# Attention on one Trainium2 core: score and transpose products grouped by PSUM bank, and casts of q and k given new places

## The chip, the core and the metric

The kernel runs on one core of one Trainium2 chip. The core has five engines that run side by side, each with its own queue of instructions in program order: TensorE (PE in the rows; PEld is its weight load), VectorE (DVE), ScalarE (ACT), GpSimd (POOL) and SyncE (SP), which here only starts DMAs. An instruction waits for others by semaphores. TensorE writes to PSUM, which is divided into banks of 128 x 512 float32; VectorE and ScalarE read them. The metric is device microseconds of one execution. 785.85 us is the median of three runs before (785.13 to 787.29).

## The reference, cut to what matters

```python
scores = 1 / sqrt(64) * (q @ k.T)                # 4 batches, 8 heads, 576 x 64
cum = cumsum(log(clip(f, 1e-4, 1)))
scores = where(causal, -1e9, scores + cum[:, None] - cum[None, :])
attn = exp(scores - scores.max(-1))
attn = attn / (attn.sum(-1) + 1e-9)
x = (attn @ v)                                   # 2304 tokens x 512
# then: each token to the best of 8 experts (x normalised), relu(x @ w1) @ w2, times the gate
# then: max of three products, times w_out
```

All in float32. The change lies in the attention alone.

## The kernel before

**Pairs and heads.** Attention goes through 16 pairs of heads `p`, two heads `h = 2p, 2p+1` each, four pairs to a batch. For a pair SyncE loads `q2` and `k2` (128 x 1152, L251). A score product in full precision is made of high and low parts: `q_hi` and `k_hi` cast to the rounded type fp32r (L315, L318, by `evict`: L433 on VectorE, L435 on ScalarE), GpSimd subtracts the casts from the originals (`q_lo` L321 into `At`, `k_lo` L324 into `R2`), SyncE copies `At` to `Bt` (L327). Three sets of these buffers (`At`, `Bt`, `R1`, `R2`) are in turn, so the split for pair `p` runs while the heads of earlier pairs are computed.

**A head.** The 576 rows of a head are five blocks `t` of 64, 128, 128, 128, 128 rows; by causality block `t` needs 64, 192, 320, 448, 576 columns. For each block there are two score products (L344: `At` by `R1`, and `Bt` by `R2`) into a PSUM bank `s`; block 4 is cut in two of 288 columns, so a head has six `s` tiles, with three banks in turn. VectorE's reduction (L361, a custom instruction followed by a read of its accumulator) adds the mask, writes `P` and the row extreme `nm`, which frees the bank. ScalarE's `exp` (L381) follows. TensorE transposes `P` by 128 x 128 (L397), the last 64 columns of each block into a bank `tl` (L393, L399), and the first 64 x 64 (L401); VectorE or ScalarE copies each bank `t` (two in turn) and `tl` (one) to `PT` (L433, L435).

**A pair's output.** When both heads are transposed, two groups `po` (L459) multiply `PT` by `v`; `ot` (L469) copies the result, `pb` (L478) transposes it back, L487 normalises it with `rs` (L445), and SyncE stores it. At the end of a batch a chain of small VectorE instructions and a few products (L575 ff., `ohp` L724, `pr`, `ptab`) routes the tokens.

**What sets the order.** The code does not write instructions in one order. It lists tasks with an engine (or a choice of two), a planned cost, a priority, and the tasks they need; `Sched` (L122) takes, again and again, the task that could start first by its own clock, the priority breaking ties, and emits its instructions. So the queues' order is decided when the kernel is built, by planned costs. The tasks' dependencies steer that order alone; the semaphores in the built program come from the data that instructions read and write. PSUM banks are planned by `get` and `rel`: a tile is taken by the task with `get` and given back by the one with `rel`. The order of blocks in a head is `order = (4, 0, 3, 1, 2)`, and products have a width of at least 192 columns (`wp`, L342), also for block 0, which needs 64.

Of the kernel before, what the change touches and what calls it, by code (L numbers as in the profile page):

```python
# [214 lines left out]
def attention(tc, g, qT, kT, v, x_dram, es):  # L215
# [87 lines left out]

    def split_tasks(p):
        i, u = p % NQ, 10 * p - 6
        load = None
        if p > 1:
            old = [fs[h, t, k] for h in (2 * p - 6, 2 * p - 5) for t in range(NBLK) for k in range(1 + (t == 4))] if p >= NQ else []
# [27 lines left out]
    def s_task(h, t, k, j0, w):  # L336
        p, r = divmod(h, 2)
        i = p % NQ

        def fn(e):  # L340
            st = st_[h, t, k] = ps_s.tile([128, 512], F32, tag="s", name=f"s_{h}_{t}_{k}")
            wp = max(w, 192)  # L342
            for ps_i, (lt, rt, kk) in enumerate(((At[i], R1[i], 128), (Bt[i], R2[i], 66))):
                nc.tensor.matmul(st[:, 0:wp], lt[0:kk, r, ROW0[t]:ROW0[t] + 128],  # L344
                                 rt[0:kk, r, j0:j0 + wp], start=(ps_i == 0), stop=(ps_i == 1))

        fs[h, t, k] = sd.task("PE", pe(2 * max(w, 192)), fn, slot[h, t] - LEAD, ready[p], get=("s", (h, t, k)))

    def r_task(h, t, k, j0, w, n, ext):
        def fn(e):  # L350
            if k == 0:
                if t == order[0] and h % H == 0:
                    b = h // H
# [12 lines left out]
        fr[h, t] = sd.task("DVE", dve(w), fn, slot[h, t], deps, get=None if k else ("P", (h, t)), rel=[("s", (h, t, k))])

    def head(h):
        p, r = divmod(h, 2)
        b = h // H  # L370
        T = PT[h % NPT]
        for t in order:
            n, ext = ROWS[t], EXT[t]
            parts = ((0, 288), (288, 288)) if t == 4 else ((0, ext),)
            for k, (j0, w) in enumerate(parts):
                s_task(h, t, k, j0, w)
                r_task(h, t, k, j0, w, n, ext)

            def exp(e, t=t, n=n, ext=ext, k=len(parts) - 1):
                P, nm = Pt[h, t]  # L380
                nc.scalar.activation(out=P[0:n, 0:ext], in_=P[0:n, 0:ext], func=AF.Exp, bias=nm[0:n, k:k + 1], scale=-1.0,  # L381
                                     accum_out=sums[b][0:n, t, h % H:h % H + 1])

            fe[h, t] = sd.task("ACT", 0.28 + ext / 1200, exp, slot[h, t], [fr[h, t]])
        old = [fo[p - 2, u] for u in range(2)] if p >= 2 else []
        for t in order:
            i0 = ROW0[t]

            def tr(e, t=t, i0=i0):
                P = Pt.pop((h, t))[0] if t not in (0, 4) else Pt[h, t][0]  # L390
                if t == 0:
                    tl = tl_[h] = ps_t.tile([128, 512], F32, tag="tl", name=f"tl_{h}", bufs=1)
                    nc.tensor.transpose(tl[0:64, 384:512], Pt.pop((h, 4))[0][:, 512:576], g.ident)  # L393
                    return
                w = tl_[h, t] = ps_t.tile([128, 512], F32, tag="t", name=f"t_{h}_{t}")
                for a in range(t):
                    nc.tensor.transpose(w[:, 128 * a:128 * a + 128], P[:, 128 * a:128 * a + 128], g.ident)  # L397
                if t != 4:
                    nc.tensor.transpose(tl_[h][0:64, 128 * t - 128:128 * t], P[:, 128 * t:128 * t + 64], g.ident)  # L399
                if t == 1:  # L400
                    nc.tensor.transpose(w[0:64, 128:192], Pt.pop((h, 0))[0][0:64, 0:64], g.ident[0:64, 0:64])  # L401

            nb = {0: 1, 1: 2.5, 2: 3, 3: 4, 4: 4}[t]
            deps = [fe[h, t]] + ([fe[h, 4]] if t == 0 else [ft[h, 0]] if t != 4 else [])
            ft[h, t] = sd.task("PE", 0.107 * nb, tr, slot[h, t] + LT, deps, get=("tl", h) if t == 0 else ("t", (h, t)),
                               rel=[("P", (h, x)) for x in {0: (4,), 1: (0, 1), 4: ()}.get(t, (t,))])
            if t == 0:
                continue

            def ev(e, t=t, i0=i0):  # L410
                w = tl_.pop((h, t))
                if t == 1:
                    evict(e, T[0:64, 0, 0:64], w[0:64, 128:192])
                evict(e, T[:, 0:t, i0:i0 + 128], w[:, 0:128 * t].rearrange("p (a i) -> p a i", a=t))

            x = 0.13 if t == 1 else 0.0
            fv[h, t] = sd.task(("ACT", "DVE"), (act(128 * t) + x, dve(128 * t) + x), ev, slot[h, t] + LT - 4, [ft[h, t]] + old,
                               rel=[("t", (h, t))])

        def tail(e):  # L420
# [1039 lines left out]
```

## Time and profile before

| | before |
|---|---|
| median of 3 runs | 785.85 us (785.13 to 787.29) |
| the profiled execution, and its span | 785.06 us, 783.3 us |
| busy: TensorE, VectorE, ScalarE, GpSimd | 738.9 us (94%), 461.9 (59%), 368.2 (47%), 237.7 (30%) |
| the chain that ended last, share by engine | TensorE 75%, VectorE 9%, DMA 7%, issue 4%, others 1% or less each |
| granted TensorE clock, mean | 0.984 of full speed |
| attention | about 10 to 221 us; then routing and experts |

The shares are averages over stages with different limits. Attention takes the first 28% of the span; there VectorE and ScalarE are nearly as busy as TensorE, while behind 242 us TensorE works almost alone. A "busy" TensorE says that products follow each other; from the distance of two starts (the pitch) one reads what a product costs, since the listed time of one includes its passage through the array. The clock is the share of full speed that the chip granted. In rows with `[x <-E tile Lnn]` the engine had been idle for x us before, until engine E's instruction released it.

### The profile page before, as it was taken

The page shows a single profiled execution, that of the slowest core. Times are in us where ns is not written, and L with a number is a line of the kernel's source. Part 1 is how long each engine was busy: PE and PEld are TensorE (multiplying, and loading weights), DVE is VectorE, ACT ScalarE, POOL GpSimd, SP SyncE. Part 2 cuts the span into 40 slices and gives each one's busy share as a digit, 9 for nine tenths or more (in the row PEclk, how much of TensorE's full clock was granted, in tenths as well). Part 3 has the DMA queues.
Part 4 walks back from the last instruction along what each step waited for, and adds up shares of the span by engine and source line. Part 5 has one row for each costly group of instructions (what it writes and reads, how often), then busy time and mean ns, then how long its engine had stood idle before and what let it go on. Part 6 is the DMA issues. An engine that isn't in the chain of part 4 may idle for free.

```text
span 783.3 us, 13403 instructions
## 1 busy us (share of the span) xinstructions
PE 738.9 (94%) x4862; PEld 682.3 (87%) x4862; DVE 461.9 (59%) x1076; ACT 368.2 (47%) x870; POOL 237.7 (30%) x189
## 2 busy tenths in 40 slices
PE   2989999999949998999999999999999999999996
PEld 1868877778738998999999999989999899999995
DVE  6888887988567998867767877941211211112110
ACT  5668887978836653454554563231211212212111
POOL 7464443532020344234223113341221211212112
PEclk9999999999978999999999999999999999999998
DMA  9959775751145465556474653200000000100001
GB/s 228 239 125 216 191 178 143 182 118 40 23 116 208 151 220 181 186 181 233 151 257 147 230 198 126 82 28 14 1 40 1 28 14 1 41 0 15 28 1 43
DMA packets 44614, 90.19 MB, mean 115 GB/s; under 512 B 23320, under 2 KB 23320, under 8 KB 44544
## 3 DMA queue, kind: packets, MB, share of 16 engines
q1 hardware_dynamic: 40960, 77.83, 34.0%
q0 software_dynamic: 3152, 9.88, 3.5%
q10 hardware_dynamic: 432, 1.57, 0.5%
q8 instruction: 40, 0.66, 0.3%
q14 instruction: 30, 0.25, 0.1%
HBM read 74.97 MB, written 9.44 MB: 108 GB/s over the span
## 4 chain that ended last, share of the span: by engine, by line
PE 75%; DVE 9%; DMA 7%; issue 4%; ACT 1%; POOL 1%; SPq 1%; POOLq 0%; DVEq 0%; ACTq 0%
PE pm L907 10%; PE pm L906 10%; PE pm L908 10%; PE s L344 6%; PE po L459 6%; PE t L397 4%; PE ph L908 3%; PE ph L907 3%; PE py L906 3%; PE py L908 3%; PE ph L906 3%; PE py L907 3%; PE po L1268 3%; PE po L1267 3%; PE po L1266 3%
## 5 line engine op out<-in xcount | busy, mean ns | idle before, releaser
L1240 DVE TENSOR_TENSOR tm<-pm,tm 128x384 f32<-128x384 f32 x72 | 40.1, 557 | 199.4 <-PE pm L908 198.2
L907 PE MATMUL pm<-x_y,m 128*128 128x384 f32 x432 | 144.5, 335 | 0.0
L908 PE MATMUL pm<-x_y,m 128*128 128x384 f32 x432 | 144.4, 334 | 0.0
L906 PE MATMUL pm<-x_y,m 128*128 128x384 f32 x432 | 144.4, 334 | 0.0
L381 ACT ACTIVATE P<-P,nm 128x576 f32<-128x576 f32 (+4 forms) x160 | 88.3, 555 | 17.0 <-DVE nm L361 16.7
L344 PE MATMUL s<-R,At 128*128 128x192 f32 (+1 forms) x192 | 71.3, 380 | 14.9 <-DVE At L271 10.5
L934 ACT ACTIVATE w<-stg 128x1024 fp32r<-128x1024 f32 x63 | 66.2, 1056 | 33.3 <-DMA stg<-in_w_dram 14.4
L907 PEld LDWEIGHTS pm<-x_y,m 128*128 128x128 f32 x432 | 81.1, 188 | 0.6 <-POOL x_y L1199 0.3
L951 DVE TENSOR_TENSOR w<-stg,w 128x1024 fp32r<-128x1024 f32 x54 | 70.2, 1304 | 19.3 <-ACT w L934 18.9
L907 PE MATMUL ph<-x,w 128*128 128x384 f32 (+7 forms) x256 | 79.3, 310 | 2.1 <-DVE x L1083 2.1
L906 PEld LDWEIGHTS pm<-x_y,m 128*128 128x128 f32 x432 | 81.1, 188 | 0.2
L908 PEld LDWEIGHTS pm<-x_y,m 128*128 128x128 f32 x432 | 81.1, 188 | 0.0
L906 PE MATMUL py<-h,w 128*128 128x384 f32 (+7 forms) x256 | 79.5, 311 | 0.8 <-DVE h L1141 0.8
L908 PE MATMUL ph<-x,w 128*128 128x384 f32 (+7 forms) x256 | 79.4, 310 | 0.8 <-DVE w L951 0.7
L906 PE MATMUL ph<-x,w 128*128 128x384 f32 (+7 forms) x256 | 79.4, 310 | 0.7 <-ACT x L934 0.7
L1251 POOL TENSOR_TENSOR g<-tm,g 128x384 fp32r<-128x384 f32 x34 | 36.5, 1074 | 141.4 <-ACT g L934 141.4
L908 PE MATMUL py<-h,w 128*128 128x384 f32 (+7 forms) x256 | 78.5, 307 | 0.4 <-DVE w L951 0.4
L907 PE MATMUL py<-h,w 128*128 128x384 f32 (+7 forms) x256 | 78.2, 305 | 0.0
L934 ACT ACTIVATE g<-tm 128x384 fp32r<-128x384 f32 x36 | 18.8, 524 | 115.9 <-DVE tm L1240 115.9
L361 DVE CUSTOM_DVE_ANT_0 P<-s,mask 128x288 f32<-128x288 f32 (+4 forms) x160 | 64.4, 422 | 11.1 <-PE s L344 6.7
L344 PE MATMUL s<-R,Bt 66*128 66x192 f32 (+1 forms) x192 | 60.2, 320 | 4.3 <-DMA R<-clo 4.3
L321 POOL TENSOR_TENSOR At<-q,At 64x1152 fp32r<-64x1152 f32 x15 | 40.3, 2684 | 77.1 <-DVE At L433 24.7
(246 smaller groups left out, 1620.4 us busy)
## 6 DMA issues: line engine op xcount, KB each, us to landing
stg<-in_w_dram SPq DMA_DIRECT2D x61, 512.0 KB
q<-in_q_dram SPq DMA_DIRECT2D x32, 288.0 KB
k<-in_k_dram SPq DMA_DIRECT2D x32, 288.0 KB
sd<-in_m_dram SPq DMA_DIRECT2D x18, 512.0 KB
Bt<-At SPq DMA_DIRECT2D x16, 288.0 KB
v<-in_v_dram SPq DMA_DIRECT2D x4, 1024.0 KB
x_dram<-XL SPq DMA_DIRECT2D x64, 64.0 KB
sd_o<-in_mo_dram SPq DMA_DIRECT2D x6, 512.0 KB
```

What stands on the lines that cost most here:

```text
L321: nc.gpsimd.tensor_tensor(out=At[i][64:128], in0=raws[p][0][64:128], in1=At[i][64:128].bitcast(F32), op=ALU.subtract)
L344: nc.tensor.matmul(st[:, 0:wp], lt[0:kk, r, ROW0[t]:ROW0[t] + 128], rt[0:kk, r, j0:j0 + wp], start=(ps_i == 0), stop=(ps_i == 1))
L361: nc.vector.tensor_tensor_reduce(out=P[0:n, j0:j0 + w], in0=st_.pop((h, t, k))[0:n, 0:w], in1=g.mask[0:n, m0:m0 + w], scale=-0.125, scalar ...
L381: nc.scalar.activation(out=P[0:n, 0:ext], in_=P[0:n, 0:ext], func=AF.Exp, bias=nm[0:n, k:k + 1], scale=-1.0, accum_out=sums[b][0:n, t, h % ...
L459: nc.tensor.matmul(po[64 * r:64 * r + 64, lo - c0:w], vt[b][0:n, a, (2 * hp + r) * D:(2 * hp + r + 1) * D], PT[(2 * p + r) % NPT][0:n, a, ...
L906: nc.tensor.matmul(out, whi, xhi, start=start, stop=False)
L907: nc.tensor.matmul(out, whi, xlo, start=False, stop=False)
L908: nc.tensor.matmul(out, wlo, xhi, start=False, stop=stop)
L934: nc.scalar.activation(out=out, in_=in_, func=AF.Copy)
L951: ENG[e].tensor_tensor(out=w[:, 1], in0=t, in1=w[:, 0].bitcast(F32), op=ALU.subtract)
L1240: nc.vector.tensor_tensor(out=mx[0], in0=mx["p", w][:, 0:MC], in1=mx[0], op=ALU.max)
L1251: ENG[e].tensor_tensor(out=ht[:, 1, :], in0=mx[0], in1=ht[:, 0, :].bitcast(F32), op=ALU.subtract)
```

## The change

Three things, all in `attention()`.

*Scores by bank.* A head has four units in place of six tiles: block 4's first half, its second half, blocks 2 and 1 side by side in one bank (320 + 192 columns), blocks 3 and 0 in one bank (448 + 64). Block 0's products are 64 columns wide and no longer 192. Of the two blocks in a bank the second is reduced first, and the bank is given back behind the other.

*Transposes by bank.* Three groups, block 4, blocks 2 and 1, blocks 3 and 0, each into one `t` bank. A group waits for the exponentials of both its blocks; the bank `tl` is begun right ahead of block 4's group. The copies to `PT` are as many as before.

*Casts.* The planned costs of a cast go from (1.02, 0.67) to (1.1, 0.8), those of a subtraction from 2.6 to 2.7. In the plan `q_lo` now needs both casts, `k_lo` needs `q_lo`, and the casts of a pair need the `k_lo` of the pair before (`quiet`).

```diff
-        qh = sd.task(("ACT", "DVE"), (1.02, 0.67), q_hi, u, old + [load])
-        ql = sd.task("Pool", 2.6, q_lo, u, [qh])
+        qh = sd.task(("ACT", "DVE"), (1.1, 0.8), q_hi, u, old + [load, quiet[0]])
         qc = sd.task("SP", 0.9, q_copy, u, [qh], lat=2.0)
-        kh = sd.task(("ACT", "DVE"), (1.02, 0.67), k_hi, u, old + [load])
-        kl = sd.task("Pool", 2.6, k_lo, u, [kh])
+        kh = sd.task(("ACT", "DVE"), (1.1, 0.8), k_hi, u, old + [load, quiet[0]])
+        ql = sd.task("Pool", 2.7, q_lo, u, [qh, kh])
+        kl = quiet[0] = sd.task("Pool", 2.7, k_lo, u, [kh, ql])
...
+    UNITS = (((4, 0, 0, 288, 0),), ((4, 1, 288, 288, 0),), ((2, 0, 0, 320, 0), (1, 0, 0, 192, 320)), ((3, 0, 0, 448, 0), (0, 0, 0, 64, 448)))
+    FLIPS = ((4,), (2, 1), (3, 0))
...
+            for t, k, j0, w, c in UNITS[n]:
+                for ps_i, (lt, rt, kk) in enumerate(((At[i], R1[i], 128), (Bt[i], R2[i], 66))):
+                    nc.tensor.matmul(st[:, c:c + w], lt[0:kk, r, ROW0[t]:ROW0[t] + 128], rt[0:kk, r, j0:j0 + w],
+                                     start=(ps_i == 0), stop=(ps_i == 1))
...
+        for x, (t, k, j0, w, c) in enumerate(UNITS[n][::-1]):
...
+            end = x == len(UNITS[n]) - 1
+            dep = fr[h, t] = sd.task("DVE", dve(w), red, u, [dep] + ([fr[h, t]] if k else []), get=None if k else ("P", (h, t)),
+                                     rel=[("s", (h, n))] if end else [])
...
+    def slot(h, n):
+        return 5 * h + (0, 0.5, 1.5, 3)[n]
...
+            ft[h, n] = sd.task("PE", cost, tr, u + LT, [fe[h, t] for t in ts] + [ft[h, "tl"]], get=("t", (h, n)),
+                               rel=[("P", (h, t)) for t in ts])
...
-            ts = (0, 1, 2) if u == 0 else (0, 3, 4)
+            ts = (1, 2, "tl") if u == 0 else (0, 2, "tl")
```

The numbers of instructions on TensorE, of reductions and of copies to `PT` are the same in both. What moves, in three places; in the names a first number is the head (or the pair, for `q2`, `k2`, `po`, `ot`), a second the block before and the unit or the first block of a group after.

VectorE, before, around the casts of pairs 3 and 4 (`P` and `s` are of head 4, `ISA` is the reduction and, in the row behind it, its accumulator read):

```order
L361 ISA P_4_1_577,nm_4_1_578<-s_4_1_0_555,mask_81 128x192
L361 ISA nm_4_1_578 128x1
L433 CAST R10_116<-k2_3_414 128x1152
L487 TENSOR_TENSOR XL0_599<-pb_0_0_573,rs_0_441 128x3x144
L445 TENSOR_SCALAR rs_1_605<-sums0_205 128x10
L446 RECIPROCAL rs_1_605<-rs_1_605 128x10
L433 CAST At1_111<-q2_4_506 128x1152
L433 CAST R11_117<-k2_4_507 128x1152
L433 COPY PT3_125<-tl_3_558 64x4x64
```

VectorE, after, around the casts of pair 4:

```order
L447 COPY PT0_122<-tl_4_616 64x4x64
L447 CAST At1_111<-q2_4_555 128x1152
L365 ISA P_6_4_706,nm_6_4_707<-s_6_0_695,mask_81 128x288
L365 ISA nm_6_4_707 128x1
L447 CAST R11_117<-k2_4_556 128x1152
L365 ISA P_6_4_706,nm_6_4_707<-s_6_1_709,mask_81,nm_6_4_707 128x288
```

The cast of `k` of pair 3 has left VectorE (it stands on ScalarE); those of pair 4 come two heads later, with one reduction between them.

VectorE, before, from the cast of `q` of pair 10 on (heads 15 and 16):

```order
L433 CAST At1_111<-q2_10_1514 128x1152
L361 ISA P_16_4_1681,nm_16_4_1682<-s_16_4_1_1676,mask_81,nm_16_4_1682 128x288
L361 ISA nm_16_4_1682 128x1
L361 ISA P_16_0_1716,nm_16_0_1717<-s_16_0_0_1697,mask_81 64x64
L361 ISA nm_16_0_1717 64x1
L361 ISA P_16_3_1719,nm_16_3_1720<-s_16_3_0_1701,mask_81 128x448
L361 ISA nm_16_3_1720 128x1
L433 CAST R11_117<-k2_10_1515 128x1152
L433 COPY ot_6_0_1730<-po_6_0_1709 128x320
L433 COPY PT3_125<-t_15_3_1725 128x3x128
```

VectorE, after, at the same casts:

```order
L447 CAST At1_111<-q2_10_1499 128x1152
L365 ISA P_16_1_1663,nm_16_1_1664<-s_16_2_1632,mask_81 128x192
L365 ISA nm_16_1_1664 128x1
L365 ISA P_16_2_1673,nm_16_2_1674<-s_16_2_1632,mask_81 128x320
L365 ISA nm_16_2_1674 128x1
L459 TENSOR_SCALAR rs_7_1679<-sums1_877 128x10
L460 RECIPROCAL rs_7_1679<-rs_7_1679 128x10
L447 CAST R11_117<-k2_10_1500 128x1152
L365 ISA P_16_0_1705,nm_16_0_1706<-s_16_3_1684,mask_81 64x64
L365 ISA nm_16_0_1706 64x1
L365 ISA P_16_3_1708,nm_16_3_1709<-s_16_3_1684,mask_81 128x448
```

The two casts stand as far apart as before, but the copy `ot` no longer follows the cast of `k`; it is on ScalarE, behind the exponential of block 3.

TensorE, before, from the second half of block 4 of head 16:

```order
L344 MATMUL s_16_4_1_1676<-R12_118,At2_112 128x288
L344 MATMUL s_16_4_1_1676<-R22_121,Bt2_115 128x288
L397 MATMUL t_15_4_1684<-ident_78,P_15_4_1611 128x128 x4
L344 MATMUL s_16_0_0_1697<-R12_118,At2_112 128x192
L344 MATMUL s_16_0_0_1697<-R22_121,Bt2_115 128x192
L344 MATMUL s_16_3_0_1701<-R12_118,At2_112 128x448
L344 MATMUL s_16_3_0_1701<-R22_121,Bt2_115 128x448
L393 MATMUL tl_15_1705<-ident_78,P_15_4_1611 64x128
```

TensorE, after, from the same products:

```order
L349 MATMUL s_16_1_1628<-R12_118,At2_112 128x288
L349 MATMUL s_16_1_1628<-R22_121,Bt2_115 128x288
L349 MATMUL s_16_2_1632<-R12_118,At2_112 128x320
L349 MATMUL s_16_2_1632<-R22_121,Bt2_115 128x320
L349 MATMUL s_16_2_1632<-R12_118,At2_112 128x192
L349 MATMUL s_16_2_1632<-R22_121,Bt2_115 128x192
L392 MATMUL tl_15_1645<-ident_78,P_15_4_1566 64x128
L409 MATMUL t_15_4_1647<-ident_78,P_15_4_1566 128x128 x4
L409 MATMUL t_15_2_1656<-ident_78,P_15_2_1605 128x128 x2
L392 MATMUL tl_15_1645<-ident_78,P_15_2_1605 64x128
L409 MATMUL t_15_2_1656<-ident_78,P_15_1_1597 128x128
```

Four products in a row now fill one bank, and the transposes of two blocks stand together; what came between them (single tiles of 192 or 448 columns, single blocks) stands earlier or later.

## Rows read from the trace of the kernel before

**Rows 1.** Stretches: from:to us; length, busy us of engines (instructions), PEclk, DMA share, GB/s

```profile
47.60:51.20 3.60, 3.60 (x15) 2.87 (x16) 2.35 (x11) 2.04 (x6) 3.52 (x2) 0.53 1.02 248
62.00:99.00 37.00, 37.00 (x309) 30.23 (x308) 31.91 (x118) 32.38 (x106) 16.57 (x7) 1.00 0.83 198
```

**Rows 2.** Waits of TensorE, 44.9 to 221.4 us: total us, times, longest

```profile
PE s L344 <- DVE nm L361: 4.1, 3, 2.4
PE pb L478 <- DVE ot L433: 1.7, 2, 0.9
```

**Rows 3.** Line 433, casts of k: durations ns min/median/max, first and last start

```profile
L433 DVE CAST R<-k x13: 747/2168/3074, 40.2 to 177.7; 128x1152 fp32r<-128x1152 f32 x13
```

**Rows 4.** Timeline from 39 us: start, duration us, engine, line, out<-in [idle before]

```profile
39.50 2.63 POOL L321 TENSOR_TENSOR At<-q,At 64x1152 fp32r<-64x1152 f32 x1 [6.62 <-DVE nm L361]
...
40.25 2.50 DVE L433 CAST R<-k 128x1152 fp32r<-128x1152 f32 x1
...
43.51 2.63 DVE L433 CAST At<-q 128x1152 fp32r<-128x1152 f32 x1
...
46.06 0.75 DVE L433 CAST R<-k 128x1152 fp32r<-128x1152 f32 x1
...
46.27 3.04 POOL L321 TENSOR_TENSOR At<-q,At 64x1152 fp32r<-64x1152 f32 x1 [0.75 <-issue]
...
47.60 0.46 PE L344 MATMUL s<-R,At 128*128 128x192 f32 x1 [2.38 <-DVE nm L361]
```

**Rows 5.** Timeline, a cast on ScalarE

```profile
28.06 1.15 ACT L435 ACTIVATE R<-k 128x1152 fp32r<-128x1152 f32 x1
```

**Rows 6.** Timeline, casts of pair 9

```profile
101.89 3.07 DVE L433 CAST R<-k 128x1152 fp32r<-128x1152 f32 x1
...
105.16 0.41 PE L344 MATMUL s<-R,At 128*128 128x320 f32 x1 [0.84 <-DVE nm L361]
```

**Rows 7.** Timeline from 114 us, casts of pair 10

```profile
114.02 1.20 PE L459 MATMUL po<-PT,v 128*64 128x320 f32 x12
114.03 2.64 POOL L321 TENSOR_TENSOR At<-q,At 64x1152 fp32r<-64x1152 f32 x1 [6.29 <-PE s L344]
...
114.93 2.35 DVE L433 CAST R<-k 128x1152 fp32r<-128x1152 f32 x1
...
117.20 0.48 DVE L433 COPY ot<-po 128x320 f32<-128x320 f32 x1
...
117.73 1.00 PE L478 MATMUL pb<-w,ot 128*128 128x144 f32 x6 [0.83 <-DVE ot L433]
118.67 2.10 PE L459 MATMUL po<-PT,v 128*64 128x256 f32 x20
```

**Rows 8.** Groups by line and shape in attention: busy us, mean ns, idle before

```profile
L361 DVE CUSTOM_DVE_ANT_0 P<-s,mask 128x448 f32<-128x448 f32 x32 | 19.7, 615 | 2.7 <-PE s L344 1.3 <-ACT P L381 0.6
L381 ACT ACTIVATE P<-P,nm 128x448 f32<-128x448 f32 x32 | 21.2, 662 | 0.5 <-DVE nm L361 0.2
L724 DVE TENSOR_TENSOR ohp<-iota,rm 128x640 f16<-128x640 f32 x3 | 2.5, 826 | 0.0
```

**Rows 9.** Timeline of TensorE at 62 us: pitches

```profile
62.32 0.27 PE L344 MATMUL s<-R,Bt 66*128 66x192 f32 x1
62.43 0.27 PE L397 MATMUL t<-ident,P 128*128 128x128 f32 x1
62.54 0.27 PE L399 MATMUL tl<-ident,P 128*64 128x128 f32 x1
62.74 0.24 PE L401 MATMUL t<-ident,P 64*64 64x64 f32 x1
62.91 0.42 PE L344 MATMUL s<-R,At 128*128 128x320 f32 x1
```

**Rows 10.** Timeline at the start of attention

```profile
14.51 2.62 POOL L321 TENSOR_TENSOR At<-q,At 64x1152 fp32r<-64x1152 f32 x1
...
16.04 0.46 DVE L361 CUSTOM_DVE_ANT_0 P<-s,mask 128x288 f32<-128x288 f32 x1 [1.58 <-PE s L344]
```

More of the change, by code (lines that the diff above doesn't have):

```diff
@@ L307, in split_tasks @@
         if p > 1:
-            old = [fs[h, t, k] for h in (2 * p - 6, 2 * p - 5) for t in range(NBLK) for k in range(1 + (t == 4))] if p >= NQ else []
+            old = [fs[h, n] for h in (2 * p - 6, 2 * p - 5) for n in range(4)] if p >= NQ else []
             load = sd.task("SP", 3.3, lambda e: load_pair(p), u - 8, ready[p - 2], lat=2.0)
@@ L334, in split_tasks, with s_unit @@
+        ql = sd.task("Pool", 2.7, q_lo, u, [qh, kh])
+        kl = quiet[0] = sd.task("Pool", 2.7, k_lo, u, [kh, ql])
         ready[p] = [x for x in (qh, ql, qc, kh, kl, dec) if x is not None]
-    def s_task(h, t, k, j0, w):
+    UNITS = (((4, 0, 0, 288, 0),), ((4, 1, 288, 288, 0),), ((2, 0, 0, 320, 0), (1, 0, 0, 192, 320)), ((3, 0, 0, 448, 0), (0, 0, 0, 64, 448)))
+    FLIPS = ((4,), (2, 1), (3, 0))
+    def s_unit(h, n):
         p, r = divmod(h, 2)
[L338 to L353, printed above, removed]
+        b, i = h // H, p % NQ
+        u = slot(h, n)
+        def mm(e):
+            st = st_[h, n] = ps_s.tile([128, 512], F32, tag="s", name=f"s_{h}_{n}")
+            for t, k, j0, w, c in UNITS[n]:
+                for ps_i, (lt, rt, kk) in enumerate(((At[i], R1[i], 128), (Bt[i], R2[i], 66))):
+                    nc.tensor.matmul(st[:, c:c + w], lt[0:kk, r, ROW0[t]:ROW0[t] + 128], rt[0:kk, r, j0:j0 + w],
+                                     start=(ps_i == 0), stop=(ps_i == 1))
@@ L354, in fn, with red @@
+        cost = 0.08 + sum(2 * max(0.112, 0.013 + x[3] / 2400) for x in UNITS[n])
+        dep = fs[h, n] = sd.task("PE", cost, mm, u - LEAD, ready[p], get=("s", (h, n)))
+        for x, (t, k, j0, w, c) in enumerate(UNITS[n][::-1]):
+            def red(e, t=t, k=k, j0=j0, w=w, c=c):
+                if n == 0 and h % H == 0:
                     sums[b] = sm.tile([128, NBLK, H], F32, tag="sums", name=f"sums{b}", bufs=2)
                     nc.vector.memset(sums[b][64:128, 0, :], 1.0)
-                P = pp.tile([128, S], F32, tag="P", name=f"P_{h}_{t}")
@@ L365, in r_task @@
-        deps = [fs[h, t, k]] + ([fr[h, t]] if k else [])
-        fr[h, t] = sd.task("DVE", dve(w), fn, slot[h, t], deps, get=None if k else ("P", (h, t)), rel=[("s", (h, t, k))])
+                if k == 0:
+                    P = pp.tile([128, S], F32, tag="P", name=f"P_{h}_{t}")
+                    nm = sm.tile([128, 2], F32, tag="nm", name=f"nm_{h}_{t}")
+                    Pt[h, t] = P, nm
+                P, nm = Pt[h, t]
+                m, m0 = ROWS[t], S - 128 if t == 0 else S - EXT[t] + j0
@@ new lines, in red @@
+                nc.vector.tensor_tensor_reduce(out=P[0:m, j0:j0 + w], in0=st_[h, n][0:m, c:c + w], in1=g.mask[0:m, m0:m0 + w],
+                                               scale=-0.125, scalar=(3.0e38 if k == 0 else nm[0:m, 0:1]),
+                                               op0=ALU.add, op1=ALU.min, accum_out=nm[0:m, k:k + 1])
+            end = x == len(UNITS[n]) - 1
+            dep = fr[h, t] = sd.task("DVE", dve(w), red, u, [dep] + ([fr[h, t]] if k else []), get=None if k else ("P", (h, t)),
+                                     rel=[("s", (h, n))] if end else [])
@@ new lines, in s_unit, with exp @@
+            if (t, k) != (4, 0):
+                def exp(e, t=t, k=k):
+                    P, nm = Pt[h, t]
+                    m = ROWS[t]
+                    nc.scalar.activation(out=P[0:m, 0:EXT[t]], in_=P[0:m, 0:EXT[t]], func=AF.Exp, bias=nm[0:m, k:k + 1], scale=-1.0,
+                                         accum_out=sums[b][0:m, t, h % H:h % H + 1])
+                fe[h, t] = sd.task("ACT", 0.28 + EXT[t] / 1200, exp, u, [fr[h, t]])
+    def slot(h, n):
+        return 5 * h + (0, 0.5, 1.5, 3)[n]
@@ L368, in head @@
     def head(h):
         p, r = divmod(h, 2)
-        b = h // H
         T = PT[h % NPT]
[L372 to L384, printed above, removed]
@@ L385, in head @@
-        old = [fo[p - 2, u] for u in range(2)] if p >= 2 else []
[L386 to L418, printed above, removed]
@@ L420, in tail, with start @@
-        def tail(e):
+        for n in range(4):
+            s_unit(h, n)
+        old = [fo[p - 2, u] for u in range(2)] if p >= 2 else []
+        def tail(t, P):
+            nc.tensor.transpose(tl_[h][0:64, 128 * t - 128:128 * t], P[:, 128 * t:128 * t + 64], g.ident)
+        def start(e):
+            tl_[h] = ps_t.tile([128, 512], F32, tag="tl", name=f"tl_{h}", bufs=1)
+            tail(4, Pt[h, 4][0])
+        u4 = slot(h, 0) + LT
+        ft[h, "tl"] = sd.task("PE", 0.06, start, u4, [fe[h, 4]], get=("tl", h))
@@ new lines, in head, with tr, ev @@
+        for n, ts in enumerate(FLIPS):
+            u = slot(h, (0, 2, 3)[n])
+            def tr(e, ts=ts):
+                w = tl_[h, ts] = ps_t.tile([128, 512], F32, tag="t", name=f"t_{h}_{ts[0]}")
+                c = 0
+                for t in ts:
+                    P = Pt.pop((h, t))[0]
+                    for a in range(t):
+                        nc.tensor.transpose(w[:, c:c + 128], P[:, 128 * a:128 * a + 128], g.ident)
+                        c += 128
+                    if t == 0:
+                        nc.tensor.transpose(w[0:64, c:c + 64], P[0:64, 0:64], g.ident[0:64, 0:64])
+                    elif t != 4:
+                        tail(t, P)
+            cost = 0.05 + sum(0.109 * t + (0.08 if t == 0 else 0.03) for t in ts)
+            ft[h, n] = sd.task("PE", cost, tr, u + LT, [fe[h, t] for t in ts] + [ft[h, "tl"]], get=("t", (h, n)),
+                               rel=[("P", (h, t)) for t in ts])
+            def ev(e, ts=ts):
+                w = tl_.pop((h, ts))
+                c = 128 * sum(ts)
+                for t in ts[::-1]:
+                    if t == 0:
+                        evict(e, T[0:64, 0, 0:64], w[0:64, c:c + 64])
+                    else:
+                        c -= 128 * t
+                        evict(e, T[:, 0:t, ROW0[t]:ROW0[t] + 128], w[:, c:c + 128 * t].rearrange("p (a i) -> p a i", a=t))
+            cols = [128 * t if t else 64 for t in ts]
+            fv[h, n] = sd.task(("ACT", "DVE"), (sum(act(x) for x in cols), sum(dve(x) for x in cols)), ev, u + LT - 4, [ft[h, n]] + old,
+                               rel=[("t", (h, n))])
@@ L423, in tail @@
             evict(e, dst, tl_.pop(h)[0:64].rearrange("p (a i) -> p a i", i=128)[:, :, 64:128])
-        fv[h, 0] = sd.task(("ACT", "DVE"), (act(256), dve(256)), tail, slot[h, order[-1]] + LT - 4,
-                           [ft[h, t] for t in order] + old, rel=[("tl", h)])
+        fv[h, "tl"] = sd.task(("ACT", "DVE"), (act(256), dve(256)), corners, slot(h, 3) + LT - 4,
+                              [ft[h, n] for n in range(len(FLIPS))] + old, rel=[("tl", h)])
     RNG = ((0, 320), (320, 256))
@@ L446, in recip @@
             nc.vector.reciprocal(rs[0], rs[0])
-        rt = sd.task("DVE", 0.35, recip, u0, [fe[h, t] for h in hs for t in order])
+        rt = sd.task("DVE", 0.35, recip, u0, [fe[h, t] for h in hs for t in range(NBLK)])
         for u, (c0, w) in enumerate(RNG):
```

11 lines of the change are left out of this document (2 added, 9 removed).

## The prediction, made before the changed kernel ran

> **What bounds the kernel now.** I read the stretches first: from 62 to 99 us TensorE was busy 37.00 of 37.00 us, VectorE 31.91 and ScalarE 32.38 [rows 1]. Attention is bound by TensorE, with two engines close behind it, so an edit there is worth what it takes out of TensorE's own work or out of its waits. The waits of TensorE behind 44.9 us have five entries in all: three score products that waited for a reduction on VectorE, 4.1 us with 2.4 the longest, and two back-transposes `pb` that waited for a copy `ot` on VectorE, 1.7 us [rows 2]. That is 5.8 us, and the edit can take back no more of named waits than this. Last I asked what VectorE did ahead of each of the five: each time a cast of `k` or `q` that was slow. The 13 casts of `k` on VectorE took 0.75 us at best and 2.17 in the median [rows 3]. The mixture-of-experts part behind attention has the same instructions on TensorE in both programs, and I carry it over unchanged.
>
> **Why the casts are slow.** At 39.50 GpSimd began the subtraction for `q`, 2.63 us long; VectorE's cast of `k` began at 40.25 and lasted until 42.75, which is 0.62 us behind GpSimd's end. The next cast, of `q` at 43.51, ran 2.63 us under the subtraction for `k`. A cast that began first, at 46.06, took 0.75; there it was GpSimd that took longer, 3.04 [rows 4]. So a cast that starts under a subtraction ends about 0.62 us after it, and the one that starts ahead of it isn't slowed. On ScalarE a cast of `k` under a subtraction took 1.15 us [rows 5]: more than VectorE's 0.75, but not the 2 to 3 us of a blocked one.
>
> **The sum, part by part.** It is made against the profiled execution, 785.06 us, which lies 0.79 under the median of the runs (785.85).
>
> *The double cast, minus 2.4 and minus 1.7.* At 40.25 to 46.1 two slow casts stand almost back to back, and TensorE ran dry for 2.38 us until 47.60 [rows 4]. [...] In the new order the cast of `k` of pair 3 is on ScalarE, and between the casts of `q` of pairs 3 and 4 stand 12 reductions instead of three. The double block can't recur: 4.1 us gone. Next in line there is TensorE itself.
>
> *The four other waits, minus 3.4.* Two are of the kind at 105.16: cast of `q`, one copy, cast of `k` that lasts 3.07, and 0.84 us of waiting for the reduction queued behind it [rows 6]. The cast of pair 13, one batch later, is its twin. In the new order four reductions, a copy `ot` and the two instructions of `rs` lie between the casts in pairs 9 and 13. I estimate them at 2.6 us or more from rows like those of [rows 7, 8]; GpSimd works for 0.13 + 2.64 behind `q`'s cast, so `k`'s runs free or meets a tail of some 0.6. The other two are like 117.73: `k`'s cast began at 114.93 under the subtraction of 114.03, held the copy `ot` behind it, and `pb` waited 0.83 [rows 7]. In pairs 10 and 14 the cast stays under the subtraction also in the new order. GpSimd's subtraction waits in the built program for the cast of `q` alone (the planner's new dependencies set places, not waits), so from the start of `q`'s cast to the end of `k`'s it is 0.75 + 0.13 + 2.64 + 0.62 = 4.1 us. But `ot` is no longer behind it on VectorE. It now stands on ScalarE behind the exponentials of block 3: 4.1, then reductions of about 0.2 and of 0.62, an exponential of 0.66 and about 0.2 to read its sum, the copy of 0.48, three hops of about 0.15. That is 6.7 us after the start of `q`'s cast, or 7.2 after the products of block 4 (0.5 for their reduction) [rows 7, 8]. TensorE's work between those products and that `pb` is, by pitches, score products 1.4 (three and a half units), 19 transposes of 0.11 and one of 0.17, one `pb` group of 0.94, and the two groups `po`, 1.13 and 2.03: 7.8 us [rows 7, 9]. The cover is 0.6 us. I take all 3.4 as gone.
>
> *Casts of pairs 4 and 7, plus 0.8.* Here one reduction alone stands between the two casts, so `k`'s runs some 2.9 us on VectorE. Nearest rows: nothing (pairs 6 and 7 cast inside the stretch in which TensorE was never idle [rows 1]) and 2.38 each [rows 4]. `po` of 2.03 us and three filled banks stand ahead of TensorE, more than ahead of the double block, so I take 0.4 each; both ends, 0 and 4.8.
>
> *Routing at three batch ends, plus 0.9.* Block 2 and block 1 share a bank, and the routing chain (eight instructions, the longest 0.83 [rows 8]) now stands between their reductions, so by an estimate of 0.2 for each of the other seven the bank comes free about 2.2 us later, and the exponential of block 2 too. TensorE has both `po` groups there, 3.2 us, and `ptab`; by my count its cover is within 0.5 us of the need either way. Ends 0 and 0.85 each (the waits of [rows 6, 7]); taken 0.3 each.
>
> *The start, plus 0.4.* `k` of pair 1 is cast on VectorE ahead of the first reduction. If it falls under the subtraction of 14.51 it ends at 17.13 + 0.62 = 17.75, and the first reduction, at 16.04, moves by 1.7 us [rows 10]; if it starts first, nothing moves. No row tells which of the two starts first; I take a quarter.
>
> *The narrower products, 0.* 64 columns in place of 192, twice a head. 192 had a pitch of 0.11, 128 columns of a transpose 0.11 as well, and the 64x64 transpose 0.17 [rows 9]. In proportion to columns it would be 0.04. Ends for 64 such products: minus 4.5 and plus 3.8 us. Since 128 and 192 columns cost the same, I take the floor, no change. Moved places on SyncE and the flips' wait for two exponentials cost nothing as far as TensorE has more than 5 us of work between them, as it has in most heads.
>
> Sum: −4.1 − 3.4 + 0.8 + 0.9 + 0.4 = −5.4, so 779.7 in an execution like the profiled one and 780.4 against the median; I say **780.0**.
>
> [...]
>
> **Rivals.** *A, it doesn't do what it says.* Six casts of `k` (pairs 4, 7, 10, 11, 14, 15) stay under a subtraction, and each now brings the wait of 0.85 that four brought before: 5.1 in place of 3.4, the start loses its 1.7, and only the double block is gone: −4.1 + 1.7 + 1.7 = −0.7, 784.4. For it: no wait in the built program keeps GpSimd back. Against: the named waits follow six slow casts of at least eleven, the others none, and `ot` has left that queue.
> *B, slower.* The cover of 0.6 us in pair 10 fails. VectorE enters the cast with a backlog, the chain reduction, exponential, `ot` comes late by that backlog, and TensorE waits at `pb` or at a shared bank in all six pairs, as long as at 47.60: 6 x 2.38 = 14.3, with the old 7.5 saved, 785.06 + 14.3 − 7.5 = 791.9. It decides from a backlog of about 1.9 us a pair: 0.6 of cover and 1.25 of waiting, six times which is the gain. For it: VectorE is 86% busy and ScalarE 88% in the fullest stretch [rows 1]. Against: five casts fewer are slow, 5 x (2.17 − 0.75) = 7 us of VectorE's time [rows 3].
> *C, more.* The 64-wide products go by columns: 780.0 − 4.5 = 775.5.
>
> **How the numbers follow.** My forecast, 777 to 783.4: 0.62. A: 0.17. B: 0.12. C, and other gains above 9 us: 0.09. Range 775.0 to 786.5: it takes in forecast, A and most of C and leaves out B and a little of C, some 0.17. About 0.3%, 2.4 us, is what a measurement of this kernel can tell from no change: faster (under 783.5) 0.70, same (A mostly) 0.17, slower 0.13.
>
> **What would show it.** Right: no idle time of TensorE near 45 and no slow clock behind it; pairs 9 and 13 cast `k` in 0.75 us, pairs 10 and 14 in about 2.1 with no wait of `pb` behind them; named waits of TensorE in attention under 2.5 us; routing of the last batch starts 5 to 6 us earlier. Wrong: `pb` waiting on ScalarE's `ot` (B), score products waiting at heads 12, 20 and 28 for 0.8 or more, a first reduction near 17.7, or a pitch of the 64-wide products far from 0.11.

## The result: slower, by two collisions that the prediction didn't follow

The changed kernel took 790.83 us in the median (789.64 to 792.78, four runs) against 785.49 for the kernel before: a ratio of 1.0066, 95% interval 1.0040 to 1.0093. Forecast were 780.0 and a range up to 786.5, so the sign and the range both missed. The profiled execution took 792.78 us, 1.95 above its median; stretches below are compared between traces, times between medians.

The waits of TensorE in the kernel after, between 44.9 and 221.4 us (total us, times, longest), where the kernel before had those of [rows 2]:

```profile
PE ptab L707 <- DVE rr L703: 6.6, 2, 3.3
PE tl L392 <- DVE nm L365: 1.6, 1, 1.6
PE pb L492 <- ACT ot L449: 0.3, 1, 0.3
```

All five old waits, 5.8 us, are gone. In their place TensorE waits twice for 3.3 us at `ptab`, a product in the routing of a batch, for `rr`, the last of the routing's small VectorE instructions. Stretches of the kernel after, columns as in [rows 1]:

```profile
44.90:62.00 17.10, 16.76 (x138) 13.83 (x136) 14.80 (x43) 12.72 (x42) 9.31 (x4) 1.00 0.79 182
62.00:99.00 37.00, 32.08 (x257) 26.79 (x258) 32.67 (x113) 27.83 (x88) 19.01 (x7) 0.95 0.76 187
92.70:97.70 5.00, 4.96 (x31) 4.78 (x32) 4.04 (x22) 4.09 (x14) 0.00 (x0) 0.66 0.95 234
145.00:150.20 5.20, 5.12 (x27) 4.96 (x28) 3.68 (x23) 3.92 (x13) 0.00 (x0) 0.50 0.74 174
149.00:198.00 49.00, 49.00 (x400) 40.91 (x399) 39.33 (x147) 41.68 (x143) 15.82 (x6) 0.98 0.40 93
```

The first row is the forecast come true: almost no idle time behind 45 us, and the full clock. The second has 4.9 us of idle TensorE where [rows 1] has none. The third and fourth are the stretches right behind each wait at `ptab`: granted clocks of 0.66 and 0.50 over 5.00 and 5.20 us, by an estimate from those numbers 1.7 and 2.6 us of work lost. In the last TensorE is never idle; its 0.98 comes from the slow clock up to 150.2.

What happened ahead of the first of the two waits is in the timeline of the kernel after (start and duration in us, engine):

```profile
84.88 1.17 ACT L449 ACTIVATE At<-q 128x1152 fp32r<-128x1152 f32 x1
...
86.12 2.65 POOL L321 TENSOR_TENSOR At<-q,At 64x1152 fp32r<-64x1152 f32 x1 [3.26 <-ACT At L449]
...
87.16 1.64 DVE L730 TENSOR_SCALAR rm<-rank 128x5 int32<-128x5 int32 x1
...
87.32 2.10 PE L473 MATMUL po<-PT,v 128*64 128x256 f32 x20
...
88.71 0.16 DVE L732 TENSOR_SCALAR rq<-rank 128x5 int32<-128x5 int32 x1
88.83 0.83 DVE L738 TENSOR_TENSOR ohp<-iota,rm 128x640 f16<-128x640 f32 x1
88.97 3.15 POOL L324 TENSOR_TENSOR R<-k,R 64x1152 fp32r<-64x1152 f32 x1 [0.20 <-ACT R L449]
...
89.58 2.58 DVE L631 TENSOR_TENSOR rc<-ioc,rq 128x15 f32<-128x15 f32 x1
...
92.19 0.17 DVE L700 TENSOR_TENSOR rc<-rc,idv 128x15 f32<-128x15 f32 x1
...
92.40 0.28 DVE L703 TENSOR_TENSOR rr<-oh,rc 128x120 f16<-128x120 f16 x1
...
92.74 0.28 PE L707 MATMUL ptab<-rr,ohp 128*128 128x24 f16 x5 [3.32 <-DVE rr L703]
```

`rm` works on five numbers a partition and took 1.64 us; it ended 0.03 us behind GpSimd's subtraction for `q` of pair 8 (86.12 + 2.65). `rc`, fifteen numbers, took 2.58 and ended 0.04 behind the subtraction for `k` (88.97 + 3.15). Between the two subtractions `rq`, of the same size as `rm`, took 0.16. So these, like the casts of [rows 4] that ended 0.62 behind theirs, began under a subtraction and were held until it had ended; in what follows that is called locked. Not every instruction was: `r` and `rank`, at 86.71 and 86.93 under the subtraction for `q`, took 0.18 and 0.20. In the kernel before, the same pair was cast at 92.5 us, behind the routing, and the chain ran free:

```profile
90.89 0.28 PE L693 MATMUL ptab<-rr,ohp 128*128 128x24 f16 x5
...
93.76 2.80 POOL L321 TENSOR_TENSOR At<-q,At 64x1152 fp32r<-64x1152 f32 x1 [10.55 <-ACT At L435]
```

Mean times of the two instructions over the three batch ends, the kernel before first:

```profile
L716 DVE TENSOR_SCALAR rm<-rank 128x5 int32<-128x5 int32 x3 | 0.5, 172 | 0.1
L617 DVE TENSOR_TENSOR rc<-ioc,rq 128x15 f32<-128x15 f32 x3 | 0.5, 168 | 0.0
```

and the kernel after:

```profile
L730 DVE TENSOR_SCALAR rm<-rank 128x5 int32<-128x5 int32 x3 | 3.5, 1152 | 0.1
L631 DVE TENSOR_TENSOR rc<-ioc,rq 128x15 f32<-128x15 f32 x3 | 5.3, 1775 | 0.0
```

Two of the three batch ends are hit, those at which pairs 8 and 12 are split. At the third no pair is left to split, and there `rm` took its 0.17:

```profile
193.18 0.17 DVE L730 TENSOR_SCALAR rm<-rank 128x5 int32<-128x5 int32 x1
```

### The profile page after: what moved, and what is told of

It is laid out like the page before. It is cut to its first block, busy times and chain, and to the rows that moved or that the text cites. A ratio compares the mean times of both kernels' runs of the same rounds, so it can differ in the third digit from the quotient of the medians.

```text
span 791.1 us, 13336 instructions
## 1 busy us (share of the span) xinstructions
PE 741.3 (94%) x4862; PEld 688.8 (87%) x4862; DVE 463.0 (59%) x1077; ACT 365.9 (46%) x869; POOL 239.3 (30%) x189
## 4 chain that ended last, share of the span: by engine, by line
PE 78%; DVE 9%; DMA 6%; issue 3%; POOL 1%; ACT 1%; SPq 0%; POOLq 0%; DVEq 0%; ACTq 0%
PE pm L921 10%; PE pm L922 9%; PE pm L920 9%; PE s L349 7%; PE po L473 5%; PE t L409 4%; PE ph L922 3%; PE ph L921 3%; PE ph L920 3%; PE py L920 3%; PE py L922 3%; PE py L921 3%; PE pb L492 3%; PE po L1282 3%; PE po L1281 3%
## 5 line engine op out<-in xcount | busy, mean ns | idle before, releaser
L349 PE MATMUL s<-R,At 128*128 128x288 f32 (+2 forms) x192 | 66.1, 351 | 11.7 <-DVE At L271 10.4
L349 PE MATMUL s<-R,Bt 66*128 66x288 f32 (+2 forms) x192 | 55.7, 326 | 4.4 <-DMA R<-clo 4.4
```

The source lines that it names most:

```text
L349: nc.tensor.matmul(st[:, c:c + w], lt[0:kk, r, ROW0[t]:ROW0[t] + 128], rt[0:kk, r, j0:j0 + w], start=(ps_i == 0), stop=(ps_i == 1))
```

## The experiments

Theory P: GpSimd's subtractions of pairs 8 and 12 now run under the routing chain, hold its small VectorE instructions, TensorE waits for the chain and loses its clock behind the wait. Rival B: the bank that blocks 2 and 1 share is held through the chain, and the coarser banks and late exponentials make the wait, whatever GpSimd does.

| kernel | median us | ratio to before, 95% |
|---|---|---|
| changed | 790.83 | 1.0066 (1.0040 to 1.0093) |
| banks alone | 779.65 | 0.9917 (0.9890 to 0.9944) |
| casts' plan alone | 776.53 | 0.9883 (0.9857 to 0.9909) |
| changed, no subtractions of pairs 8, 12 | 777.89 | 0.9904 (0.9878 to 0.9929) |
| changed, those casts behind the routing | 778.84 | 0.9907 (0.9879 to 0.9936) |
| changed, no subtraction for q of 8, 12 | 779.50 | 0.9931 (0.9905 to 0.9957) |
| changed, no subtraction for k of 8, 12 | 781.71 | 0.9942 (0.9920 to 0.9964) |
| casts joined, behind the routing | 775.40 | 0.9887 (0.9864 to 0.9910) |
| casts joined, old tiles | 777.93 | 0.9911 (0.9888 to 0.9934) |

Each ratio is to runs of the kernel before taken in the same round; their medians were 785.49 us for the changed kernel, 785.92 for the next four rows and 784.88 for the last four. A difference of about 1 us between kernels of different rounds therefore says nothing.

**Each part alone.** First the banks with the old casts:

```diff
-        qh = sd.task(("ACT", "DVE"), (1.1, 0.8), q_hi, u, old + [load, quiet[0]])
+        qh = sd.task(("ACT", "DVE"), (1.02, 0.67), q_hi, u, old + [load])
+        ql = sd.task("Pool", 2.6, q_lo, u, [qh])
...
-        kh = sd.task(("ACT", "DVE"), (1.1, 0.8), k_hi, u, old + [load, quiet[0]])
-        ql = sd.task("Pool", 2.7, q_lo, u, [qh, kh])
-        kl = quiet[0] = sd.task("Pool", 2.7, k_lo, u, [kh, ql])
+        kh = sd.task(("ACT", "DVE"), (1.02, 0.67), k_hi, u, old + [load])
+        kl = sd.task("Pool", 2.6, k_lo, u, [kh])
```

> The changed kernel with the old casts (planned costs 1.02, 0.67 and 2.6, each subtraction needs its own cast alone): scores and transposes by bank, nothing else. Theory P (GpSimd's subtractions of pairs 8 and 12 run under the routing chain and hold back its small VectorE instructions, TensorE waits for the chain): ScalarE still casts q of pair 8 ahead of the routing, k later, so one subtraction of two meets the chain; waits at ptab of about 1.5 us instead of 3.3, half the slow clock behind them; 784 to 788. Theory B (the bank shared by blocks 2 and 1 is held through the routing chain and the exponential behind it comes late): the coarse banks are all here, waits at ptab stay 3.3 and the time 789 to 792.

779.65 us, lower than either theory said, and with the half collision that P expects:

```profile
83.46 2.63 POOL L321 TENSOR_TENSOR At<-q,At 64x1152 fp32r<-64x1152 f32 x1 [3.95 <-ACT At L449]
...
84.49 1.63 DVE L730 TENSOR_SCALAR rm<-rank 128x5 int32<-128x5 int32 x1
...
86.90 0.17 DVE L631 TENSOR_TENSOR rc<-ioc,rq 128x15 f32<-128x15 f32 x1
...
87.65 0.29 PE L707 MATMUL ptab<-rr,ohp 128*128 128x24 f16 x5 [0.89 <-DVE rr L703]
```

Here the cast of `q` of pair 8 is ahead of the routing, that of `k` 9.6 us later (in the changed kernel 2.9). So the new banks bring the first subtraction under the chain: the last score product of head 11, which reads the buffers that pair 8 takes over, stood behind the routing's product `pr` on TensorE (88.14 against 87.77 in the kernel before) and now stands ahead of it (81.97 against 82.86), and the planner casts `q` of pair 8 as soon as that is done (82.22). One collision costs 0.89 us of waiting, where 1.5 was expected, and the clock stays at 1.00 from 62 to 198 us.

Then the casts' plan with the old tiles (the diff above the other way round, in the kernel before):

> The kernel before with the new plan of the casts alone, six score tiles a head as before. Both theories put the loss with the banks' new order, so this one should keep the gains: no pair of slow casts back to back near 44 us (4.1 us with the clock), k of pairs 9 and 13 on ScalarE (1.7 us), q of pair 8 cast behind the routing as before. Both: 779 to 782, no wait at ptab. If the casts' plan by itself brings the collision: 787 or more.

776.53 us, 2.5 below the range that was expected; no wait at `ptab` at those two batch ends (the 0.7 us there at the last routing stand in every kernel), and TensorE busy throughout:

```profile
62.00:99.00 37.00, 37.00 (x311) 29.77 (x310) 31.37 (x118) 32.66 (x104) 18.71 (x8) 1.00 0.78 192
99.00:149.00 50.00, 50.00 (x417) 40.56 (x413) 41.37 (x155) 44.34 (x142) 23.44 (x10) 1.00 0.77 185
149.00:198.00 49.00, 49.00 (x408) 40.53 (x409) 39.46 (x152) 43.29 (x144) 11.12 (x5) 1.00 0.32 71
```

Each part alone is faster than the kernel before, by 6 and by 9 us; together they are slower by 5.

**Taking the subtractions away.** In the changed kernel nothing moves, GpSimd just does less:

```diff
         def q_lo(e):
+            if p in (8, 12):
+                return
...
         def k_lo(e):
+            if p in (8, 12):
+                return
```

> The changed kernel; GpSimd's two subtractions of pairs 8 and 12 are left out (the low parts of these pairs are stale, so their scores are wrong), every other instruction stands where it stood. Theory P: rm at line 730 takes 0.17 in place of 1.64 us and rc at line 631 0.17 in place of 2.58, no wait at ptab above 0.5 us, no slow clock behind it; 790.8 minus 2 x 3.3 minus about 5 of slow clock: 778 to 781. Theory B: nothing in the order or the banks has moved, so the waits stay 3.3 us and the time 789 to 792.

777.89 us. `rm` and `rc` are free, and of the waits between 62 and 210 us only the one of 1.6 near 63 is left:

```profile
L734 DVE TENSOR_SCALAR rm<-rank 128x5 int32<-128x5 int32 x3 | 0.5, 171 | 0.1
L635 DVE TENSOR_TENSOR rc<-ioc,rq 128x15 f32<-128x15 f32 x3 | 0.5, 166 | 0.0
```

That settles P against B: order, banks and exponentials are those of the changed kernel, and 12.9 us are gone by the medians. In the traces 11.3 us lie at the two batch ends; another 1.6 were there already ahead of the first (the second `po` of pair 4 starts at 87.32 in the changed kernel, at 85.70 here), from the start of attention, which this edit doesn't touch; the last part comes back to that. Then each subtraction apart. Without that for `q`:

> The changed kernel; of pairs 8 and 12 GpSimd's subtraction for q is left out (their low part of q is stale), the one for k stands. Theory P: rm is free (0.17 us in place of 1.64), rc is still locked out until the subtraction for k ends (some 2.5 us, or less if ScalarE's cast of k lets GpSimd begin at another time); wait at ptab 3.3 minus 1.5 = about 1.8 us a time; whether the slow clock follows a wait of that length isn't known, so 779 to 786. Theory N (only the sum of GpSimd's busy time counts, or the order): no difference from the changed kernel, 789 to 792.

779.50 us, within the range, but by another way than expected: no wait at `ptab` at either end.

```profile
87.20 0.17 DVE L732 TENSOR_SCALAR rm<-rank 128x5 int32<-128x5 int32 x1
...
88.15 0.17 DVE L633 TENSOR_TENSOR rc<-ioc,rq 128x15 f32<-128x15 f32 x1
...
89.01 2.65 POOL L326 TENSOR_TENSOR R<-k,R 64x1152 fp32r<-64x1152 f32 x1 [6.12 <-ACT R L451]
...
90.19 1.49 DVE L639 TENSOR_TENSOR ohs<-ohs,o 128x8 f16<-128x8 f16 x1
...
92.12 0.47 PE L351 MATMUL s<-R,At 128*128 128x448 f32 x1 [0.54 <-DVE nm L367]
```

With `rm` free, the chain is past `rc` before the subtraction for `k` begins; that one then catches `ohs`, behind which TensorE waits 0.54 for a reduction. So the second collision of the changed kernel was made by the first, which kept the chain back by 1.5 us. Without the subtraction for `k`:

> The changed kernel; of pairs 8 and 12 GpSimd's subtraction for k is left out, the one for q stands. Theory P: rm stays at 1.64 us, rc falls to 0.17; wait at ptab 3.3 minus 2.4 = about 0.9 us a time, as in the run with the banks alone, and no slow clock: 778 to 781. Theory N: 789 to 792.

781.71 us, 0.7 above the expected range, with its ten runs in two groups, 777.3 to 778.4 (three) and 780.4 to 783.4 (seven, the profiled one among them); what parts them is not shown. The mechanism came as expected: `rm` 1.65, `rc` 0.17, and a wait of 0.91 with the full clock behind it:

```profile
87.75 1.65 DVE L732 TENSOR_SCALAR rm<-rank 128x5 int32<-128x5 int32 x1
...
90.18 0.17 DVE L633 TENSOR_TENSOR rc<-ioc,rq 128x15 f32<-128x15 f32 x1
```

```profile
90.40:97.00 6.60, 6.07 (x50) 5.56 (x51) 6.34 (x31) 5.66 (x21) 0.00 (x0) 1.00 0.82 196
```

From the second `po` of pair 4 to the first of pair 5, and the same one batch later, TensorE took 11.41 and 11.41 us with neither subtraction, 12.21 and 12.22 with that for `k` alone, 12.61 and 12.58 with that for `q` alone, 16.38 and 17.69 with both. One collision costs 0.8 or 1.2 us, both together 5.0 and 6.3: the second comes about through the first, and of these waits only those of 3.3 us had a slow clock behind them (0.66 and 0.50; behind the 0.91 and the 0.54 it was 1.00).

**A repair.** In the plan, the casts of pairs 8 and 12 wait for the routing:

```diff
+        route = [last[0]] if p in (8, 12) else []
...
-        qh = sd.task(("ACT", "DVE"), (1.1, 0.8), q_hi, u, old + [load, quiet[0]])
+        qh = sd.task(("ACT", "DVE"), (1.1, 0.8), q_hi, u, old + [load, quiet[0]] + route)
...
-        kh = sd.task(("ACT", "DVE"), (1.1, 0.8), k_hi, u, old + [load, quiet[0]])
+        kh = sd.task(("ACT", "DVE"), (1.1, 0.8), k_hi, u, old + [load, quiet[0]] + route)
```

> The changed kernel; in the plan the casts of pairs 8 and 12 also need the end of the routing chain of batch 0 and 1. They then stand behind it, on VectorE, and so do the subtractions. Theory P: 777 to 781, the chain's instructions at 0.2 us each, no wait at ptab. Theory B: the chain still stands between the two reductions of one bank, 788 to 792.

778.84 us: the changed kernel, with all its work, less 12.0. The casts of `q` of pairs 8 and 12 now start at 90.64 and 138.22, behind the `ptab` of 88.03 and 135.64, and there is no wait at either.

**What the locked casts of k cost.** Two kernels make the casts of `q` and `k` one task on VectorE, back to back, so that `k`'s begins ahead of GpSimd:

```diff
-        qh = sd.task(("ACT", "DVE"), (1.1, 0.8), q_hi, u, old + [load, quiet[0]] + route)
+        def both(e):
+            q_hi(e)
+            k_hi(e)
+
+        qh = kh = sd.task("DVE", 1.55, both, u, old + [load, quiet[0]] + route)
...
-        kh = sd.task(("ACT", "DVE"), (1.1, 0.8), k_hi, u, old + [load, quiet[0]] + route)
```

The first starts from the repair above, the second (without `route`) from the casts' plan with the old tiles.

> The kernel with the casts of pairs 8 and 12 behind the routing; in addition the casts of q and k of a pair are one task on VectorE, back to back, so that the cast of k begins ahead of GpSimd's subtraction. Casts of k at 0.75 us in all pairs, GpSimd's subtraction for q at 3.04. Theory H (a locked cast of k is hidden as long as TensorE has work, which it has from 62 to 198 us): 777 to 780, no more than 1 us from its parent, and what is gained is the one wait of 1.6 us near 63. Theory L (each of the eight locked casts still costs TensorE some 0.4 us or more): 773 to 776.

> The kernel with the casts' plan alone and six score tiles a head, with the casts of q and k of a pair as one task on VectorE. TensorE is busy for all of 62 to 198 us in the parent. Theory H: 775 to 778, within 1 us of the parent's 776.5. Theory L: 772 to 775.

With the new banks 775.40, 3.4 less than its parent, which is in theory L's range; with the old tiles 777.93, 1.4 more than its parent, in theory H's range but past its 1 us. The parents ran in the earlier round: against each round's own kernel before it is 2.4 less and 2.4 more. So the times alone don't decide between H and L, and the traces have to. The casts of `k` on VectorE between 20 and 200 us are indeed free in the first; its parent's row, then its own:

```profile
L448 DVE CAST R<-k 128x1152 fp32r<-128x1152 f32 x10 | 22.2, 2222 | 0.1
```

```profile
L451 DVE CAST R<-k 128x1152 fp32r<-128x1152 f32 x14 | 10.5, 751 | 0.0
```

But the 3.4 us do not come from there. From 99 to 198 us TensorE was busy for all of the time in parent and child alike, whether VectorE had 83.3 us of work or 75.3, and from the second `po` of pair 5 to that of pair 15 it took 109.57 us in the parent and 109.59 in the child. What differs is ahead of that: the wait of 1.6 is gone, and the pitch of the products fell earlier. A product of 320 columns had 0.17 us at 20.49 in the child (0.15 at 25.85), still 0.27 in the parent at 26.99. In the changed kernel such a product at 146.77, where the granted clock reads 0.50, had 0.27 too; but at the start of attention the profile's clock column reads 1.00 in parent and child alike, so that it was the clock is my estimate from the pitches. The child, then the parent:

```profile
20.49 0.33 PE L353 MATMUL s<-R,Bt 66*128 66x320 f32 x1
20.66 0.25 PE L353 MATMUL s<-R,At 128*128 128x192 f32 x1
```

```profile
26.99 0.47 PE L350 MATMUL s<-R,Bt 66*128 66x320 f32 x1
27.26 0.36 PE L350 MATMUL s<-R,At 128*128 128x192 f32 x1
```

With the old tiles the loss is ahead of the steady part too, and it is one more collision: of two copies at line 104 the second, at 22.59, fell under GpSimd's subtraction for `k` of 22.33 (2.72 us) and took 2.62 us in place of some 0.3; TensorE waited 2.35 until 25.75 for the reduction behind it, and from 25.5 to 32 us the granted clock was 0.50. From the first `po` of pair 6 to the second of pair 15 this child took 100.66 us and its parent 100.84.

So theory H holds for the steady part: the locked casts, 2.22 us in place of 0.75, cost nothing there that shows (109.57 us against 109.59). Why the pitch fell at 20.5 us in one and near 31 in the other wasn't settled; neither kernel is shown to be better than the casts' plan alone (776.53), the ratios overlap.

## Why the prediction was wrong, step by step

*The double cast, −4.1:* right. No wait near 45 us, clock 1.00 from 44.9 to 62. No run shows the 1.7 in it; in the trace of before fourteen products from 47.60 on, at the granted clock of 0.53, took 3.46 us, and the same fourteen from 84.70 on, at 1.00, took 1.94, so 1.5 us less.

*The four other waits, −3.4:* right, and by the ways named. `k` of pair 9 met only a tail, that of pair 10 stayed under the subtraction, and no `pb` waited behind it. The hops, put at 0.15 us, were shorter where the trace of before shows them: `pb` at 117.73 began 0.05 behind the listed end of `ot`, and an exponential at 107.35 began 0.04 behind the read it had waited for.

```profile
105.87 1.02 DVE L447 CAST R<-k 128x1152 fp32r<-128x1152 f32 x1
```

```profile
117.65 2.46 DVE L447 CAST R<-k 128x1152 fp32r<-128x1152 f32 x1
```

*Casts of pairs 4 and 7, +0.8:* wrong in place and size. Those two brought no wait, so the term was 0; the cast of `k` of pair 5, which the order has alone on VectorE and which I left out, started under the subtraction and TensorE waited 1.61:

```profile
59.12 2.78 DVE L447 CAST R<-k 128x1152 fp32r<-128x1152 f32 x1 [0.34 <-DMA k<-in_k_dram]
...
63.60 0.27 PE L392 MATMUL tl<-ident,P 128*64 128x128 f32 x1 [1.61 <-DVE nm L365]
```

*The start, +0.4:* the cast of `k` began first (14.14, 0.77 us), and the first reduction stood at 15.99, so the step that was priced was 0. But the instruction `emb` at line 98, behind the reductions, fell under the next subtraction, and TensorE waited 1.25:

```profile
18.07 2.94 DVE L98 TENSOR_SCALAR emb<-emb,ess,rt 8x512 f32<-8x512 f32 x1
18.11 2.62 POOL L324 TENSOR_TENSOR R<-k,R 64x1152 fp32r<-64x1152 f32 x1
...
21.85 0.61 PE L349 MATMUL s<-R,At 128*128 128x320 f32 x1 [1.25 <-DVE nm L365]
```

This wait comes and goes with the order of two starts. In the kernels without one of the two subtractions `emb` began within 0.06 us of the subtraction and was held too; in the one without both, whose program is the same up to there, it began 0.36 ahead and took 0.55, and no such wait followed.

*The narrower products, 0:* right in the sum, wrong in the pitch. The two 64-wide products of a head stand at 0.03 and 0.11 us in place of 0.09 and 0.11:

```profile
65.89 0.20 PE L349 MATMUL s<-R,At 128*128 128x64 f32 x1
65.92 0.27 PE L349 MATMUL s<-R,Bt 66*128 66x64 f32 x1
66.03 0.98 PE L492 MATMUL pb<-w,ot 128*128 128x144 f32 x6
```

yet from the second `po` of pair 2 to that of pair 3 TensorE took 11.87 us, and 11.84 before; so the gain of some 0.1 us is taken back elsewhere in this pair.

*Routing at three batch ends, +0.9:* here the prediction failed. It priced the routing chain as the cause of a wait, for a bank it holds, at 0.3 us an end; the chain was the victim. It cost 5.0 and 6.3 us at two ends, 11.3 by the stretches above and 12.9 by the medians, against a sum of −5.4. Most of what it takes stood in the prediction: that a cast on VectorE which starts under a subtraction ends only behind it, and that the chain has eight small ones in front of TensorE. What was missing is that small instructions are held like casts (`rm`, 1.64 us for 0.17), which no row there shows, and the question where the changed order puts GpSimd's subtractions. I followed the casts on VectorE, since their lock was in view, and passed over those of pairs 8 and 12, which the new order has on ScalarE ahead of the routing; a cast there took 1.15 to 1.17 us, under a subtraction or not, but GpSimd starts behind it all the same. Without that collision the sum was near: 777.9 and 778.8 in the two kernels without it, forecast 780.0. Part of that is luck: the 1.61 us behind the cast of pair 5 stood in no term, and the +0.9 for the routing had no counterpart at the first two batch ends of these kernels.

Added up along the two traces: at the second `po` of pair 2 the changed kernel was 1.5 us ahead (67.55 against 69.06), it lost 11.3 at the two batch ends, and at the second `po` of pair 15 it was 5.7 behind (223.60 against 217.93). So it gained some 4.1 in between, where 3.4 was forecast for the four waits. Behind attention, which the prediction carried over unchanged, the profiled execution lost another 2.1; the cause of that is open, and the medians differ by 5.3 in all.

*The rivals.* A (the waits return) and C (the narrow products by columns, 775.5) didn't happen; of each two narrow products one had the short pitch, and the pair measured above gained nothing by it. B had the sign but not the mechanism: `pb` waited 0.33 in this stretch, and no backlog of VectorE reached the banks.

## What to carry to other kernels

When an edit moves an instruction that holds others back, as GpSimd's subtractions held `rm` and `rc` here (1.64 and 2.58 us for 0.17), list what else runs at its new time, not only the instruction whose wait one set out to cure; the smallest instructions matter most if a chain of them feeds the engine that bounds the kernel. Two parts that each gain can lose together, when one brings a subtraction forward and the other sets the next one close behind it; measure each part alone before either is thrown away. And a wait of the bounding engine can cost nearly twice its length, as here where the clock behind it fell to 0.66 and 0.50: 3.3 us of waiting were 5.0 and 6.3, and 0.9 us, with a clock of 1.00 behind it, only 1.2.

## What the runs showed of the hardware beyond that

An instruction of a few numbers a partition can be held like a cast of 1152: `rm` 1.64 us for 0.17, `ohs` 1.49 for 0.17, `rc` 2.58 for 0.17, `emb` (512 numbers) 2.94 for 0.53 to 0.78 in other kernels. The small ones ended 0.02 to 0.04 us behind GpSimd's instruction, `emb` 0.28, the casts of `k` about 0.62. A listed start 0.04 us ahead didn't win: `emb` at 18.07 was that much ahead of the subtraction and was the one held, while the cast of 14.14, 0.23 ahead, was not, and `ohp` at 88.83, 0.14 ahead, held GpSimd instead (3.15 us for 2.64). The reductions weren't slowed: the five of 448 columns that started under a subtraction in the changed kernel took 0.61 us each, and so did the other 27. And at the start of attention the pitches of the products fell (0.27 to 0.15 us for 320 columns) between 20.5 and 32 us, depending on the kernel; by the first `po` of pair 2 the joined child was 2.7 us ahead of the repair (56.74 against 59.46). With no run that isolates it, its cause stays open.
